# One masked step for the sign and low bits of the MLP's weights, and the low halves' subtraction shared out anew

## The chip, the cores and the metric

The kernel runs on one core of a Trainium2 chip. The metric is the device time of one execution in microseconds, as the median of several runs. The engines are TensorE (PE, its weight loads PEld), VectorE (DVE), ScalarE (ACT), GpSimd (POOL) and SyncE (SP), which issues most transfers. Each works through its own queue in order.

## What is computed

The reference chains three stages. Attention: 4 batches, 8 heads, 576 positions, 64 columns a head; half of the heads see the last 32 positions, the others every 32nd. Then an MLP over the 2304 tokens with 512 columns and 2048 hidden units, and then 8 experts of 1024 hidden units, of which each token takes one:

```python
def _moe_ref(x, w_in, w_out, alpha):
    h = x @ w_in
    g = np.maximum(h, 0.0) + alpha * np.minimum(h, 0.0)
    return g @ w_out
...
    e_idx = np.argmax(x @ w_gate, axis=1)
    ...
    h = np.maximum(x[mask] @ w1[e], 0.0)
    out[mask] = gate_w[mask, None] * eom[mask, e, None] * (h @ w2[e])
```

`w_in` and `w_out` are given as float64. The kernel reads the eight bytes of each number as they are and makes float32 numbers of them on the chip; this is the decoding that the change touches.

## The kernel before

**The MLP.** The hidden units are cut into 16 chunks of 128 (`NC1`), the tokens into 6 blocks of 384 (`NBLK`). For block `blk` and chunk `c` the step n = 16 blk + c makes `h` from the tokens (`mlp_in`, L439 to L441, on two PSUM banks `h`), applies the activation (`mlp_act`: L448 and L449 on ScalarE, L450 on VectorE), splits the result into a high and a low part (`mlp_split`: `gh` on ScalarE, L459, `gl` on VectorE, L460) and multiplies it with the second matrix (`mlp_out`, L473 to L475, on three accumulators). Every product is made of three: high by high, high by low, low by high. `mlp_in` and the activation run two steps ahead of `mlp_out`.

**The weights.** Chunk c of both matrices comes as one tile `raw` of 128 x 1024 float64 (1 MB, `load_w`, L391): columns 0 to 511 belong to `w_in`, 512 to 1023 to `w_out`. Each number is two 32-bit words, the low one (`words(c)[0]`) and the high one (`words(c)[1]`). Decoding takes four steps. `decode_a` (L402, ScalarE) copies the high word into a tile `stage`, scaled as a float32 by a power of two, which keeps its mantissa bits as they are. `decode_b` (VectorE) shifts the result left by 3 (L406) and brings in the top 3 bits of the low word, shifted right by 29 (L407). `decode_s` (L413, VectorE) brings in the sign from the high word. `decode_c` copies the result, rounded to the matrix format, into the high half of the tile `w` (L421, ScalarE), and GpSimd subtracts it for the low half (L422). `stage` has three buffers. The same kind of subtraction serves the experts' weights later (L886 to L888).

**The order** is written out by hand (`manual_schedule`): each engine's queue is the order of the calls. In 13 passes ahead of the loop (`NPRO`), attention's groups 0 to 9 are worked off, and chunk k's decoding starts in pass 2 + 2k and goes on by one step a pass (`T0`, chunks 0 to 4; `DEC` is 4). Then come the first two activations, and then the loop over n. In its first 12 passes, pass n ends the decoding of chunk n + 4, does `decode_b` and `decode_s` of chunk n + 5 and `decode_a` of chunk n + 6. In the same block attention's groups 10 to 22 go on, one in most passes. For a group, `att_scores` writes two banks (L228, L234), `att_max` takes maxima on VectorE (L252), `att_exp` makes exponentials on ScalarE (L278, L281), `att_norm` makes reciprocals on VectorE (L295, L296) and products on GpSimd (L297; one group on VectorE), `att_transpose` turns them on TensorE (L313, in the loop into bank `T`; read by L315), `att_values` multiplies with `v` (L328, in the loop into bank `T` as well) and `att_store` and `att_rest` split the result (`xh` on ScalarE, L367, `xl` on VectorE, L372). After the first block the weights stay in place.

Routing and the experts follow in the last block and behind it.

Of the kernel before, what the change touches and what calls it, by code (L numbers as in the profile page):

```python
# [7 lines left out]
F32 = mybir.dt.float32  # L8
F32R = mybir.dt.float32r
BF16 = mybir.dt.bfloat16  # L10
I32 = mybir.dt.int32
AF = mybir.ActivationFunctionType
ALU = mybir.AluOpType
X = mybir.AxisListType.X
# [9 lines left out]
NC1 = FF // P  # L24
# [18 lines left out]
DEC = 4  # L43
# [19 lines left out]
RS = 7  # L63
NEG = -1.0e9
BIG = 12582912.0
SIGN = -(2**31)

C_ID = 0
C_I8 = C_ID + P
# [14 lines left out]
def attention_prelu_mlp_routed_experts_kernel(  # L84
# [11 lines left out]
    nc = tc.nc  # L96
# [28 lines left out]
    with tc.manual_schedule():  # L125
# [144 lines left out]
        def att_exp(gi):  # L270
# [6 lines left out]
            if b < PE_MASK:  # L277
                nc.scalar.activation(out=nm[:r, : 2 * nj], in_=nm[:r, : 2 * nj], func=AF.Copy, scale=SCALE)  # L278
            for u in range(2 * nj):
# [3 lines left out]
                    in_=src,  # L283
                    func=AF.Exp,
                    bias=nm[:r, u : u + 1],
# [18 lines left out]
        def att_transpose(gi, tag):  # L304
# [9 lines left out]
            ptt = apool.tile([P, 4, P], F32, tag="pt", name="ptt", bufs=NPT_BUFS)  # L314
            nc.scalar.activation(out=ptt[:kk, :nu, :r], in_=tr[:kk, :nu, :r], func=AF.Copy)  # L315
            pt_t[gi] = ptt
# [20 lines left out]
        def att_store(gi):  # L337
# [28 lines left out]
            for src, dh, dl in moves:  # L366
                nc.scalar.activation(out=dh, in_=src, func=AF.Copy)  # L367
            px_t[gi] = moves
# [8 lines left out]
        raw_t, w_t = {}, {}  # L377

        def stage():
            return xpool.tile([P, 2 * (DM + 1)], F32, tag="stage", name="stage", bufs=3)  # L380
# [3 lines left out]
        def w_tile(c, dt, name):  # L384
            return wpool.tile(
                [P, 2048], dt, tag="wa" if c < NA else "wb", name=name, bufs=NA if c < NA else NC1 - NA
            )

        def load_w(c):
            raw_t[c] = w_tile(c, I32, "raw64")  # L390
            nc.sync.dma_start(raw_t[c], wp[c].bitcast(I32))  # L391


        dec_t = {}

        def words(c):
            two = raw_t[c].rearrange("p (n two) -> p n two", two=2)
            return two[:, :, 0], two[:, :, 1]

        def decode_a(c):  # L400
            t = dec_t[c] = stage()[:, :1024]
            nc.scalar.activation(out=t, in_=words(c)[1].bitcast(F32), func=AF.Copy, scale=2.0**-112)  # L402

        def decode_b(c):
            t = dec_t[c].bitcast(I32)
            nc.vector.tensor_scalar(out=t, in0=t, scalar1=3, scalar2=None, op0=ALU.logical_shift_left)  # L406
            nc.vector.scalar_tensor_tensor(  # L407
                out=t, in0=words(c)[0], scalar=29, in1=t, op0=ALU.logical_shift_right, op1=ALU.bitwise_or
            )

        def decode_s(c):
            t = dec_t[c].bitcast(I32)
            nc.vector.scalar_tensor_tensor(  # L413
                out=t, in0=words(c)[1], scalar=SIGN, in1=t, op0=ALU.bitwise_and, op1=ALU.bitwise_or
            )
            raw_t.pop(c)

        def decode_c(c):
            t = dec_t.pop(c)
            w = w_t[c] = w_tile(c, F32R, "w")  # L420
            nc.scalar.activation(out=w[:, :1024], in_=t, func=AF.Copy)  # L421
            nc.gpsimd.tensor_tensor(out=w[:, 1024:], in0=t, in1=w[:, :1024].bitcast(F32), op=ALU.subtract)  # L422

        def w_in(c, part, k):
            return w_t[c][:, part * 1024 + k * P : part * 1024 + (k + 1) * P]
# [29 lines left out]
        def mlp_split(n):  # L455
            v = h_t.pop(n)
            gh = xpool.tile([P, BLK], F32R, tag="gh", name="gh", bufs=3)
            gl = xpool.tile([P, BLK], F32R, tag="gl", name="gl", bufs=2)
            nc.scalar.activation(out=gh, in_=v, func=AF.Copy)  # L459
            nc.vector.tensor_tensor(out=gl, in0=v, in1=gh.bitcast(F32), op=ALU.subtract)  # L460
            g_t[n] = (gh, gl)
# [606 lines left out]
        def load_ws(k):  # L1068
            for _, c in zip(range(k), loads):
                load_w(c)  # L1070
# [49 lines left out]
        steps_done = {}  # L1120

        def decode(k, n):

            steps = [decode_a, decode_b, decode_s, decode_c]
            for f in steps[steps_done.get(k, 0) : n]:
                f(k)
            steps_done[k] = max(steps_done.get(k, 0), min(n, 4))

        for s in range(NPRO):
            att_step(s, ("h", "h") if s % 2 else ("S", "X"), "acc0" if s % 2 else "T", "acc1" if s % 2 else "acc2")  # L1130
# [4 lines left out]
            if s == 4:  # L1135
# [3 lines left out]
                    out=wg_hl[:, :, 2 * E :], in0=wg_sb, in1=wg_hl[:, :, : 2 * E].bitcast(F32), op=ALU.subtract  # L1139
                )  # L1140
                nc.vector.memset(acc_oh[:, 0, :], 0.0)
            for k in range(NC1):
                n = s - (T0[k] if k < len(T0) else 99)
                if n >= 0:
                    decode(k, n + 1)

        span[:] = [FIRST + EXTRA if EXTRA < LV else 0, NG]
        decode(DEC, 3)
        decode(DEC + 1, 1)
        for n in range(2):  # L1150
            mlp_in(n, range(KD - 1, KD))
            mlp_act(n)
            mlp_split(n)
        last = NBLK * NC1
        turn_at, logits_at = {}, {}
        for blk in range(NBLK - 1):
            for j in range(TPB):
                c = 2 * j + 1 if blk < NBLK - 2 else j
# [11 lines left out]
        for n in range(last):  # L1170
            blk, c = divmod(n, NC1)
            todo = []
            if blk + 1 < len(steps_of) and c < NC1 - 2:
                s0, s1 = steps_of[blk + 1]
                k = s1 - s0
                todo = list(range(s0 + k * c // (NC1 - 2), s0 + k * (c + 1) // (NC1 - 2)))
            for s in todo[:-1]:
                att_step(s, ("S", "X"), "T", "T")
            s = todo[-1] if todo else -9
            if on(s - 1):  # L1180
                att_exp(s - 1)
                att_norm(s - 1)
            if n + 2 < last:
                mlp_in(n + 2)
            if on(s - LV):
                att_values(s - LV, "T")
                att_store(s - LV)
            att_back(s)
            if n + 2 < last:
                mlp_act(n + 2)  # L1190
            if n + DEC < NC1:
                decode(n + DEC, 4)
            att_front(s)
            if on(s):
                att_scores(s, ("S", "X"))
                att_max(s)
            if n + DEC + 1 < NC1:
                decode(n + DEC + 1, 3)
            mlp_out(n, range(1))
            if on(s - LT):  # L1200
                att_transpose(s - LT, "T")
            mlp_out(n, range(1, 2))
            if (blk - 1, c) in logits_at:
                logits(blk - 1, logits_at[blk - 1, c])
            if (blk - 1, c) in turn_at:
                turn(blk - 1, turn_at[blk - 1, c])
            if blk > 0 and c == (7 if blk < NBLK - 1 else 4):
                gather_logits(blk - 1)
                rest = route_parts(blk - 1)
                next(rest)  # L1210
            if blk > 0 and c == (8 if blk < NBLK - 1 else 5):
                next(rest, None)
            if blk > 0 and c == (9 if blk < NBLK - 1 else 6):
                rank(blk - 1)
            mlp_out(n, range(2, TPB))
            load_ws(1)
            if n + DEC + 2 < NC1:
                decode(n + DEC + 2, 1)
            if n + 2 < last:
                mlp_split(n + 2)  # L1220
            if c == NC1 - 1 and blk == 3:
                s_a.close()
                epool = s_x.enter_context(tc.tile_pool(name="epool", bufs=1))
                idx_in = epool.tile([P, NSLOT], I32, name="idx_in")
                idx_out = epool.tile([P, NSLOT], I32, name="idx_out")
                idx_any = epool.tile([1, 1], I32, name="idx_any")
                e_i32 = epool.tile([1, NSLOT], I32, name="e_i32")
                taken = epool.tile([P, NTT], F32, name="taken")
                used = epool.tile([P, E], F32, name="used")
                nc.vector.memset(taken, 0.0)  # L1230
            if blk == NBLK - 1:
                if c == 6:
                    for _ in plan_parts(True):
                        pass
                    load_expert(0, 0)
                    load_expert(0, 1)
                if c == EL:
                    lists(True)
                    indices(True)
                if c in (9, 10, 11):  # L1240
                    gathers(0)
                if c == 11:
                    split_expert(0, 0)
                    load_expert(1, 0)
                if c == 13:
                    turn_x(0, 0)
                if c == 14:
                    turn_x(0, 1, bank("X"))
                    gathers(2)
                    split_expert(1, 0)  # L1250
                    load_expert(2, 0)
                if c == 15:
                    turn_x(1, 0)
            if c == NC1 - 1:
                evacuate(blk)
# [236 lines left out]
```

## Time and profile before

| | |
|---|---|
| median of 3 runs | 828.43 us (828.38 to 828.44) |
| profiled execution | 827.54 us, its span 825.8 us |
| granted TensorE clock, mean | 0.978 |
| TensorE busy | 783.3 us, 95% |
| VectorE busy | 465.1 us, 56% |
| ScalarE busy | 427.6 us, 52% |
| GpSimd busy | 223.9 us, 27% |

The profile shows one execution. A row of a timeline has the start and the duration in us, the engine, the line of the kernel (L406), the operation, its output and inputs by the program's names, their shapes, and in brackets the idle time of the engine just before it with what ended it. A busy time counts from an instruction's start to its end, with any time in which it stands still in between. Instructions of one engine can overlap by about 0.1 us at their ends. The granted clock is given as a share of TensorE's full 2.4 GHz. Rows with "..." between them leave lines out.

### The profile page before, as it was taken

The numbers are of one execution on the slowest core, as the hardware profiler recorded it, in microseconds if no ns is written. First come the engines' busy times: TensorE is split into PE (matmuls) and PEld (weight loads), VectorE is DVE, ScalarE is ACT, GpSimd is POOL, SyncE is SP. The second block draws the span as 40 slices with busy tenths as digits, with TensorE's granted clock in tenths as the row PEclk, the third lists the DMA queues.
The fourth block names the chain that finished last, engine by engine and source line by source line (L and its number), as shares of the span: only waits on it lengthen the run. The fifth ranks groups of instructions, "written<-read, shape, count | busy, mean of one in ns | idle before, by whom it ended". The sixth has DMA issues, their size and how long they took to land. (4 is left out here: it accounts for less than half of the span.)

```text
span 825.8 us, 13693 instructions
## 1 busy us (share of the span) xinstructions
PE 783.3 (95%) x5035; PEld 659.0 (80%) x5035; DVE 465.1 (56%) x980; ACT 427.6 (52%) x1057; POOL 223.9 (27%) x152
## 2 busy tenths in 40 slices
PE   7778889999999999999999999999989998999996
PEld 4566767888888888888898898889879876878884
DVE  4979997345544454556333434657695447854422
ACT  6847676445544454555333333265534656655542
POOL 2734444011100011111000000113474465546422
PEclk9789899999999999999999999999999999999998
DMA  9707411111200121101000100553224577787421
GB/s 342 303 1 298 167 56 49 33 33 46 84 18 1 47 87 64 36 11 39 2 1 1 39 1 1 204 191 125 56 90 159 176 268 250 281 290 270 161 88 41
DMA packets 22621, 91.04 MB, mean 110 GB/s; under 512 B 3082, under 2 KB 7312, under 8 KB 15376
## 3 DMA queue, kind: packets, MB, share of 16 engines
q1 hardware_dynamic: 18816, 78.52, 26.8%
q0 software_dynamic: 3728, 11.55, 4.0%
q8 instruction: 41, 0.67, 0.3%
q14 instruction: 36, 0.29, 0.1%
HBM read 105.78 MB, written 9.97 MB: 140 GB/s over the span
## 5 line engine op out<-in xcount | busy, mean ns | idle before, releaser
L439 PE MATMUL h<-xh,w 128*128 128x384 f32 x384 | 131.2, 342 | 4.1 <-DVE gl L460 3.8
L440 PE MATMUL h<-xl,w 128*128 128x384 f32 x384 | 130.5, 340 | 0.7 <-DVE xl L372 0.7
L441 PE MATMUL h<-xh,w 128*128 128x384 f32 x384 | 130.4, 340 | 0.0
L450 DVE SCALAR_TENSOR_TENSOR h<-h,nalpha,a 128x384 f32<-128x384 f32 x96 | 59.9, 624 | 116.1 <-ACT h L449 116.0
L473 PE MATMUL acc<-w,gh 128*128 128x512 f32 x288 | 125.3, 435 | 0.0
L297 POOL TENSOR_TENSOR p<-p,sm 96x512 f32<-96x512 f32 (+2 forms) x47 | 48.2, 1026 | 283.6 <-DVE sm L296 260.5
L888 DVE TENSOR_TENSOR wx<-raw,wx 128x1024 fp32r<-128x1024 f32 x72 | 97.1, 1392 | 46.9 <-ACT wx L886 46.6
L475 PE MATMUL acc<-w,gl 128*128 128x512 f32 x288 | 114.3, 397 | 0.0
L474 PE MATMUL acc<-w,gh 128*128 128x512 f32 x288 | 114.1, 396 | 0.0
L448 ACT ACTIVATE a<-h 128x384 f32<-128x384 f32 x96 | 47.2, 491 | 105.9 <-PE h L441 105.9
L886 ACT ACTIVATE wx<-raw 128x1024 fp32r<-128x1024 f32 x96 | 94.6, 1056 | 7.6 <-DMA raw<-in_wexp_dram 7.6
L1042 PE MATMUL acc<-wx,hh 128*128 128x512 f32 x304 | 97.0, 401 | 0.0
L888 POOL TENSOR_TENSOR wx<-raw,wx 128x1024 fp32r<-128x1024 f32 x24 | 63.1, 2629 | 90.7 <-ACT wx L886 90.6
L439 PEld LDWEIGHTS h<-xh,w 128*128 128x128 f32 x384 | 73.4, 191 | 9.6 <-DVE gl L460 5.5
L440 PEld LDWEIGHTS h<-xl,w 128*128 128x128 f32 x384 | 73.2, 191 | 4.8 <-DVE xl L372 1.0
L441 PEld LDWEIGHTS h<-xh,w 128*128 128x128 f32 x384 | 73.2, 191 | 0.0
L460 DVE TENSOR_TENSOR gl<-h,gh 128x384 fp32r<-128x384 f32 x96 | 53.3, 555 | 33.0 <-PE acc L475 18.2
L895 POOL DMA_INDIRECT xg<-rows,idx_in x23 | 29.3, 1274 | 145.4 <-ACT h L449 139.0
L1042 PEld LDWEIGHTS acc<-wx,hh 128*128 128x128 f32 x304 | 56.6, 191 | 11.2
L475 PEld LDWEIGHTS acc<-w,gl 128*128 128x128 f32 x288 | 54.6, 190 | 13.2
L459 ACT ACTIVATE gh<-h 128x384 fp32r<-128x384 f32 x96 | 46.7, 486 | 34.8 <-DVE h L450 34.7
L473 PEld LDWEIGHTS acc<-w,gh 128*128 128x128 f32 x288 | 54.5, 189 | 10.6 <-issue 0.3
(259 smaller groups left out, 1548.3 us busy)
## 6 DMA issues: line engine op xcount, KB each, us to landing
raw<-in_wexp_dram SPq DMA_DIRECT2D x64, 1024.0 KB
raw<-in_wp_dram SPq DMA_DIRECT2D x16, 1024.0 KB
qk<-in_qkv_dram SPq DMA_DIRECT2D x10, 576.0 KB
rows<-stage SPq DMA_DIRECT2D x15, 256.5 KB
v<-in_qkv_dram SPq DMA_DIRECT2D x8, 320.0 KB
qk<-in_qkv_dram SPq DMA_DIRECT2D x4, 384.0 KB
v<-in_qkv_dram SPq DMA_DIRECT2D x6, 256.0 KB
qk<-in_qkv_dram SPq DMA_DIRECT2D x4, 224.0 KB
```

The lines of the kernel that those rows point to most:

```text
L297: (nc.vector if gi in NRV else nc.gpsimd).tensor_tensor(out=pt[:r, :nu, :kk], in0=pt[:r, :nu, :kk], in1=sm[:r, :nu].unsqueeze(2).to_broadc ...
L439: mm(ph[:, :BLK], w_in(c, 0, k), xh[:, k, :], start=(k == 0), stop=False)
L440: mm(ph[:, :BLK], w_in(c, 0, k), xl[:, k, :], start=False, stop=False)
L441: mm(ph[:, :BLK], w_in(c, 1, k), xh[:, k, :], start=False, stop=(k == KD - 1))
L450: nc.vector.scalar_tensor_tensor(out=v, in0=v, scalar=nalpha[:, c : c + 1], in1=a, op0=ALU.mult, op1=ALU.add)
L460: nc.vector.tensor_tensor(out=gl, in0=v, in1=gh.bitcast(F32), op=ALU.subtract)
L473: mm(o, gh[:, t], w_out(c, 0), start=(c == 0), stop=False)
L474: mm(o, gh[:, t], w_out(c, 1), start=False, stop=False)
L475: mm(o, gl[:, t], w_out(c, 0), start=False, stop=(c == NC1 - 1))
L886: nc.scalar.activation(out=w[:, :1024], in_=raw, func=AF.Copy)
L888: eng.tensor_tensor(out=w[:, 1024:], in0=raw, in1=w[:, :1024].bitcast(F32), op=ALU.subtract)
L1042: mm(po[i], h[:, h0 : h0 + P], wk[:, w0 : w0 + 512], start=st, stop=sp)
```

## The change

`decode_b` no longer reads the low word as 32 bits. A shift on 16-bit parts takes the second 16 bits of each number, shifts them right by 13 and writes the 3 bits over the low 16 bits of the high word in `raw` itself (`decode_a` has read that word before). The shift left by 3 stays. `decode_s` then takes the sign and the 3 bits from the high word with one mask, in one instruction as before. So VectorE's L407, on 1024 words, gives way to a 16-bit instruction on 1024 elements, and L413 keeps its form with another constant.

The low half is made in two parts by a new function `low`. For chunks 0 to 3, VectorE subtracts all 1024 columns, in a fifth step `decode_d`, one pass after `decode_c`. For chunks 4 to 15, GpSimd subtracts the columns of `w_out` in `decode_c`, and VectorE those of `w_in` in `decode_d`, which stands in pass n behind `mlp_out` and `load_ws`, ahead of `decode_a` of chunk n + 6 and of `mlp_split`. The calls `decode(DEC, 3)` and `decode(DEC + 1, 1)` move from ahead of the first two activations to behind them.

```diff
--- before.py
+++ after.py
@@ -9,6 +9,7 @@
 F32R = mybir.dt.float32r
 BF16 = mybir.dt.bfloat16
 I32 = mybir.dt.int32
+U16 = mybir.dt.uint16
 AF = mybir.ActivationFunctionType
 ALU = mybir.AluOpType
 X = mybir.AxisListType.X
@@ -63,7 +64,7 @@
 RS = 7
 NEG = -1.0e9
 BIG = 12582912.0
-SIGN = -(2**31)
+SIGN_AND_TAIL = -(2**31) + 7
 
 C_ID = 0
 C_I8 = C_ID + P
...
@@ -403,23 +406,34 @@
 
         def decode_b(c):
             t = dec_t[c].bitcast(I32)
+            q = raw_t[c].bitcast(U16).rearrange("p (n four) -> p n four", four=4)
+            nc.vector.tensor_scalar(
+                out=q[:, :, 2], in0=q[:, :, 1], scalar1=13, scalar2=None, op0=ALU.logical_shift_right
+            )
             nc.vector.tensor_scalar(out=t, in0=t, scalar1=3, scalar2=None, op0=ALU.logical_shift_left)
-            nc.vector.scalar_tensor_tensor(
-                out=t, in0=words(c)[0], scalar=29, in1=t, op0=ALU.logical_shift_right, op1=ALU.bitwise_or
-            )
 
         def decode_s(c):
             t = dec_t[c].bitcast(I32)
             nc.vector.scalar_tensor_tensor(
-                out=t, in0=words(c)[1], scalar=SIGN, in1=t, op0=ALU.bitwise_and, op1=ALU.bitwise_or
+                out=t, in0=words(c)[1], scalar=SIGN_AND_TAIL, in1=t, op0=ALU.bitwise_and, op1=ALU.bitwise_or
             )
             raw_t.pop(c)
 
+        def low(eng, c, a, b):
+            w = w_t[c]
+            eng.tensor_tensor(
+                out=w[:, 1024 + a : 1024 + b], in0=dec_t[c][:, a:b], in1=w[:, a:b].bitcast(F32), op=ALU.subtract
+            )
+
         def decode_c(c):
-            t = dec_t.pop(c)
             w = w_t[c] = w_tile(c, F32R, "w")
-            nc.scalar.activation(out=w[:, :1024], in_=t, func=AF.Copy)
-            nc.gpsimd.tensor_tensor(out=w[:, 1024:], in0=t, in1=w[:, :1024].bitcast(F32), op=ALU.subtract)
+            nc.scalar.activation(out=w[:, :1024], in_=dec_t[c], func=AF.Copy)
+            if c >= DEC:
+                low(nc.gpsimd, c, 512, 1024)
+
+        def decode_d(c):
+            low(nc.vector, c, 0, 512 if c >= DEC else 1024)
+            dec_t.pop(c)
 
         def w_in(c, part, k):
             return w_t[c][:, part * 1024 + k * P : part * 1024 + (k + 1) * P]
@@ -1121,10 +1135,10 @@
 
         def decode(k, n):
 
-            steps = [decode_a, decode_b, decode_s, decode_c]
+            steps = [decode_a, decode_b, decode_s, decode_c, decode_d]
             for f in steps[steps_done.get(k, 0) : n]:
                 f(k)
-            steps_done[k] = max(steps_done.get(k, 0), min(n, 4))
+            steps_done[k] = max(steps_done.get(k, 0), min(n, 5))
 
         for s in range(NPRO):
             att_step(s, ("h", "h") if s % 2 else ("S", "X"), "acc0" if s % 2 else "T", "acc1" if s % 2 else "acc2")
@@ -1145,12 +1159,12 @@
                     decode(k, n + 1)
 
         span[:] = [FIRST + EXTRA if EXTRA < LV else 0, NG]
-        decode(DEC, 3)
-        decode(DEC + 1, 1)
         for n in range(2):
             mlp_in(n, range(KD - 1, KD))
             mlp_act(n)
             mlp_split(n)
+        decode(DEC, 3)
+        decode(DEC + 1, 1)
         last = NBLK * NC1
         turn_at, logits_at = {}, {}
         for blk in range(NBLK - 1):
@@ -1214,6 +1228,8 @@
                 rank(blk - 1)
             mlp_out(n, range(2, TPB))
             load_ws(1)
+            if n + DEC < NC1:
+                decode(n + DEC, 5)
             if n + DEC + 2 < NC1:
                 decode(n + DEC + 2, 1)
             if n + 2 < last:
```

## Rows read from the trace of the kernel before

**Rows 1.** the page's busy us, share of the span and count, by engine:

```profile
PE 783.3 (95%) x5035; PEld 659.0 (80%) x5035; DVE 465.1 (56%) x980; ACT 427.6 (52%) x1057; POOL 223.9 (27%) x152
```

**Rows 2.** busy us by stretch, granted clock, DMA share, GB/s:

```profile
51.00:55.00 4.00, 3.92 (x12) 3.92 (x13) 1.21 (x3) 0.69 (x2) 0.00 (x0) 0.50 0.00 0
...
85.00:90.00 5.00, 5.00 (x17) 4.42 (x16) 4.93 (x6) 2.82 (x8) 3.23 (x2) 0.50 0.76 310
...
113.00:121.00 8.00, 6.45 (x47) 5.07 (x43) 7.86 (x12) 5.34 (x15) 3.85 (x2) 1.00 0.15 43
...
141.00:147.00 6.00, 6.00 (x45) 4.86 (x41) 2.53 (x7) 3.55 (x14) 0.85 (x2) 1.00 0.15 44
```

**Rows 3.** TensorE's waits: us in total, times, longest; the last from 8 to 140 us:

```profile
PE T L313 <- DVE xl L372: 8.2, 7, 2.3
...
PE sl_bank L228 <- ACT p L281: 1.7, 3, 0.6
...
PE X L228 <- ACT p L281: 1.3, 3, 0.5
...
PE h L439 <- DVE gl L460: 3.7, 1, 3.7
```

**Rows 4.** timeline of VectorE, one step: start, duration, line, operands:

```profile
101.56 0.41 DVE L252 TENSOR_REDUCE nm<-X 126x2 f32<-126x252 f32 x1
...
101.88 2.65 DVE L406 TENSOR_SCALAR stage<-stage 128x1024 int32<-128x1024 int32 x1
...
104.57 1.22 DVE L407 SCALAR_TENSOR_TENSOR stage<-raw,stage 128x1024 int32<-128x1024 int32 x1
...
105.83 1.22 DVE L413 SCALAR_TENSOR_TENSOR stage<-raw,stage 128x1024 int32<-128x1024 int32 x1
...
107.44 0.16 DVE L295 TENSOR_SCALAR sm<-sm 126x4 f32<-126x4 f32 x1
...
108.78 0.41 DVE L252 TENSOR_REDUCE nm<-X 126x2 f32<-126x252 f32 x1
```

**Rows 5.** timeline of GpSimd, the same step:

```profile
101.57 2.42 POOL L422 TENSOR_TENSOR w<-stage,w 128x1024 fp32r<-128x1024 f32 x1
```

**Rows 6.** timeline of VectorE, stalls ahead of the loop and in its first pass:

```profile
24.28 2.05 DVE L295 TENSOR_SCALAR sm<-sm 126x4 f32<-126x4 f32 x1
...
32.87 0.81 DVE L295 TENSOR_SCALAR sm<-sm 126x4 f32<-126x4 f32 x1 [0.78 <-ACT p L281]
...
39.43 2.33 DVE L295 TENSOR_SCALAR sm<-sm 72x2 f32<-72x2 f32 x1
...
46.20 3.18 DVE L413 SCALAR_TENSOR_TENSOR stage<-raw,stage 128x1024 int32<-128x1024 int32 x1
...
57.55 3.34 DVE L407 SCALAR_TENSOR_TENSOR stage<-raw,stage 128x1024 int32<-128x1024 int32 x1
```

**Rows 7.** one line's instructions: shortest, median, longest in ns:

```profile
L406 DVE TENSOR_SCALAR stage<-stage x16: 675/804/2997, 14.3 to 130.6; 128x1024 int32<-128x1024 int32 x16
...
L422 POOL TENSOR_TENSOR w<-stage,w x16: 2355/2498/3350, 23.0 to 137.6; 128x1024 fp32r<-128x1024 f32 x16
...
L888 DVE TENSOR_TENSOR wx<-raw,wx x72: 1210/1220/3426, 543.8 to 807.6; 128x1024 fp32r<-128x1024 f32 x72
```

**Rows 8.** timeline of VectorE, where steps of the loop begin:

```profile
63.05 0.40 DVE L252 TENSOR_REDUCE nm<-sl_bank 96x2 f32<-96x256 f32 x1
...
137.12 0.41 DVE L252 TENSOR_REDUCE nm<-sl_bank 96x2 f32<-96x256 f32 x1
...
143.05 0.41 DVE L252 TENSOR_REDUCE nm<-sl_bank 96x2 f32<-96x256 f32 x1
...
149.23 0.41 DVE L252 TENSOR_REDUCE nm<-sl_bank 96x2 f32<-96x256 f32 x1
```

**Rows 9.** timeline of ScalarE at the moved call:

```profile
44.98 1.20 ACT L402 ACTIVATE stage<-raw 128x1024 f32<-128x1024 f32 x1
...
46.91 0.49 ACT L448 ACTIVATE a<-h 128x384 f32<-128x384 f32 x1 [0.73 <-PE h L441]
```


## The prediction

> **What bounds the kernel now.** I began with the page's busy shares: TensorE 95%, VectorE 56%, ScalarE 52%, GpSimd 27% [rows 1]. They suggest that a change on VectorE and GpSimd is worth nothing. The shares by stretch say otherwise, and this is the first thing to see: from 113 to 121 us VectorE is busy for 7.86 of 8 us and TensorE for 6.45, while from 141 to 147 us, with the weights decoded, VectorE has 2.53 of 6 and TensorE is full [rows 2]. So the change can act only in about the first 140 us; behind them TensorE is the bound and an earlier start is kept to the end.
>
> The second view is TensorE's waits between 62 and 140 us: 8.2 us for VectorE's `xl` (L372) and 1.7 and 1.3 us for ScalarE's exponentials [rows 3]. All three stand behind VectorE: the transpose needs the bank that L372 empties, and the exponentials need the maxima (L252), which VectorE does late. That is 11.2 us. Before them lies one wait of 3.7 us for `gl` (L460) [rows 3], right ahead of the stretch from 51 us. After that gap, and after the longest wait for `xl`, 2.3 us, the granted clock is 0.50, the 1.2 GHz level, for some 4 to 5 us (51 to 55, 85 to 90) [rows 2].
>
> The third view is VectorE's timeline over one step. One step of the loop runs from the maxima at 101.56 to those at 108.78: 7.22 us, with no gap [rows 4]. In it L406, the shift by 3, takes 2.65 us; its shortest is 0.675 [rows 4, 7]. It stands from just after GpSimd's L422 began (101.57, for 2.42 us) [rows 5] until 0.55 us behind its end. So 1.97 us of the 7.22 are not work: VectorE stands still while GpSimd subtracts. The same is seen on L295, L413 and L407 elsewhere, each far above its unhindered time [rows 6].
>
> The Trainium skill gives a name to that (SBUF, section Who interferes with whom): VectorE and GpSimd share one pair of ports, held for a whole instruction by whoever comes first; the trace agrees by 2.65 us against 0.675.
>
> **The change, part by part: one step of the loop.** Per chunk, GpSimd's subtraction shrinks from 1024 columns to 512; its price lies between 1.18 us (half of the shortest, 2.355) and 2.36 (nothing gained) [rows 7]. The work is plain streaming, so I take 1.25.
>
> VectorE loses L407, 1.26 us from start to next start [rows 4], and the stall, 1.97. What is left of its step is 7.22 - 1.97 - 1.26 = 3.99 us. It gains half of the subtraction: 1.21 for 1024 columns in the expert stage [rows 7], so between 0.61 and, with a fixed part, 0.68; I take 0.65. That makes 4.64. The new half stands behind L413 and ahead of `gl` (L460); its input from ScalarE is ready long before, since GpSimd starts from the same copy some 5 us earlier [rows 4, 5].
>
> The unknown is the 16-bit shift, x. No row shows a 2-byte operand at an 8-byte step. Below, the dense shift L406: 0.72 from start to start without its stall. Nearest is L407 itself: it reads words of the same tile at the same 8-byte step, 1.22 us [rows 4]. An upper end I take from that row doubled, 2.46, should two-byte writes cost twice. Which port it takes matters too. At 1.23 without the shared ports it fills the time in which GpSimd holds them: GpSimd starts 0.31 us ahead of VectorE's decoding [rows 4, 5] and has 0.94 left, so L406 behind it waits for nothing and the step is 4.64 + 1.23 = 5.87 us. At 0.72 with the ports it waits those 0.94: 4.64 + 0.72 + 0.94 = 6.30 us. The ends nearly cancel, which is why I trust the sum more than either price.
>
> By the Trainium skill (VectorE: DVE Perf Modes, section What auto-detection actually checks) one source and a destination in SBUF with an even count suffice for the two-port mode, whatever the step; that would be the case of 6.30, and no run here shows it yet.
>
> **TensorE's floor.** Ten steps run from 63.05 to 137.12 us, 7.41 each [rows 8]. Less the 11.2 us of waits [rows 3] and half of the 5 us at 0.50 [rows 2], they hold 60.4 us of TensorE's own, 6.04 each; the step without decoding, 143.05 to 149.23, takes 6.18 [rows 8]. So TensorE's floor is about 6.1, VectorE's 5.87 to 6.30. With two engines that close I take the larger, 6.3. The loop gives 10 x (7.41 - 6.3) = 11.1 us; between 13 at TensorE's floor and, with x at 2.46 (a step of 7.1), 3.
>
> **The part ahead of the loop.** Here chunks 0 to 3 are subtracted on VectorE wholly, 4 x 1.21 = 4.8 us more on its queue, ahead of the next chunk's L413 and, in the last pass, of the first activation (L450). What goes are four stalls behind L422: L295 2.05, 0.81 and 2.33 us for 0.16, and L413 3.18 for 1.22 [rows 4], together 1.89 + 0.65 + 2.17 + 1.96 = 6.7 [rows 6]. GpSimd's softmax products (L297) no longer queue behind L422, which helps TensorE, but I price that at nothing since VectorE is the fuller queue there. At x = 1.23 the shift costs what L407 did. So 6.7 - 4.8 = 1.9 us gained before the loop; from 0 (VectorE stalls behind L297 instead) to 4 (x = 0.72 on five chunks as well). In the loop's first pass L407 stands 3.34 us for 1.23 [rows 6]: 2.1 of stall become some 0.6, and 0.65 of subtraction comes in: 0.9 gained. Together 2.8.
>
> The moved calls: `decode(DEC, 3)` does nothing at either place, since the passes before have done those steps; `decode(DEC + 1, 1)` is one ScalarE copy, at 44.98, that ends before the activation at 46.91 starts, which waits for TensorE [rows 9]. Behind both activations it meets a ScalarE that waits for TensorE's next product. Without that cover it would cost its 1.2 us once. Nothing else in the queues moves; SP's loads keep their order, and follow TensorE's earlier release of the buffers.
>
> **Sum.** 11.1 + 2.8 = 13.9 us. The profiled execution took 827.54 us, 0.9 under the median 828.43; 827.54 - 13.9 = 813.6, so 814.5 as a median.
>
> **The rivals.** (a) VectorE stays the bound: GpSimd's half hardly shrinks, or begins later and meets L406 or L413 with its full length, a stall of about 1 us a step. For it: L407 and L413 are hit as well as L406 [rows 6]. Against: the shift ahead of them lengthens the head start. A step of 6.9, 5.1 from the loop, 1.9 before: 821.5. (b) More than the sum: TensorE at its floor, 10 x 1.3 = 13, and the gap before 51 us closes enough that its stretch at 0.50 goes, 2 us: with 2.8, 17.8, 810.6. Against: about 2 us of that gap remain, and a wait on `xl` of little over 2 us was enough for the drop at 85 us. (c) The other side: two-byte writes into four-byte words are slow. The loop gives 10 x (7.41 - 4.64 - x) and the part before it 2.8 - 5 x (x - 1.23), which is nothing together at x = 2.4 us; beyond, the kernel is slower. At 3.7, three times the nearest row, it loses 9.3 + 9.6 = 19: 847. For it: no row shows such a write. Against: at that step L407 and L413 read in 1.22 us [rows 4] what the dense L888 reads in 1.21 at best [rows 7]. (d) Nothing changes: x about 2.4, gains and costs cancelling, 828.
>
> **How the numbers follow.** The forecast (812 to 818) 0.62; (a) 0.16; (b) 0.13; (c) 0.06; (d) 0.03. The range 810 to 821 takes in (b), the forecast and most of (a). Over 0.2%, 1.7 us, is what a measurement of this kernel can tell: faster 0.91, within it 0.03, slower 0.06.
>
> **What would show it.** Right: the new shift lasts 0.7 (with a stall) or about 1.2 us; GpSimd's subtraction about 1.25, twelve of them; maxima 6.1 to 6.4 us apart in the loop; TensorE's wait for `xl` under 3 us; no 0.50 at the place of 85 us; the first L450 about 2 us earlier. Wrong: the shift above 2 us; L406 or L413 still near 2 to 3 us; VectorE still full with steps above 6.7; or steps bounded by a ScalarE wait that the queue of before hid.

## The result and the profile after

The changed kernel takes 819.62 us as the median of four runs (819.08 to 820.06) against 828.43. That is 8.8 us less, where 13.9 were forecast; 819.62 lies inside the stated range. The ratio, of the means of the runs, is 0.9885 (95% interval 0.9862 to 0.9907); that of the medians is 0.9894, since a fourth run of the kernel before took 831.42. The profiled execution took 819.41 us with a span of 817.6. Lines are numbered anew: the shift left is L413 now (was L406), the masked step L417 (L413), the subtraction L424 on either engine (L422), the activation L464 (L450), `xl` L373 (L372), the maxima L253 (L252), the transpose L314 (L313). The new 16-bit shift is L410.

Busy time by stretch of the kernel after (stretch, its length, busy us of PE, PEld, DVE, ACT and POOL, granted clock, DMA share, GB/s):

```profile
51.00:55.00 4.00, 4.00 (x18) 3.64 (x16) 1.10 (x3) 2.45 (x4) 0.00 (x0) 0.79 0.00 0
80.00:84.00 4.00, 4.00 (x15) 3.42 (x14) 3.97 (x5) 2.82 (x8) 2.51 (x2) 0.58 1.02 424
...
113.00:121.00 8.00, 7.82 (x56) 5.86 (x53) 7.90 (x19) 7.05 (x20) 2.18 (x3) 1.00 0.20 53
130.00:136.00 6.00, 6.00 (x44) 4.86 (x43) 2.89 (x9) 3.37 (x14) 1.04 (x1) 1.00 0.16 48
```

VectorE is still full while weights are decoded, 7.90 of 8 us from 113 to 121, but TensorE now has 7.82 there against 6.45 in [rows 2]. From 130 us on VectorE is free and TensorE full. A stretch mostly at the 1.2 GHz level remains: the granted clock is 0.58 from 80 to 84 us.

TensorE's waits in the loop, 58 to 140 us (total, times, longest):

```profile
PE T L314 <- DVE xl L373: 5.2, 6, 2.4
PE X L229 <- ACT p L282: 0.7, 2, 0.4
PE sl_bank L229 <- ACT p L282: 0.5, 1, 0.5
```

The wait for `xl` is 5.2 us against 8.2 [rows 3]; its longest, 2.4 us, stands right ahead of the stretch at 0.58.

VectorE's timeline, one row of an earlier step and parts of two steps of the loop:

```profile
66.88 2.54 DVE L410 TENSOR_SCALAR raw<-raw 128x1024 uint16<-128x1024 uint16 x1
...
73.31 0.41 DVE L253 TENSOR_REDUCE nm<-X 126x2 f32<-126x252 f32 x1
73.64 1.34 DVE L410 TENSOR_SCALAR raw<-raw 128x1024 uint16<-128x1024 uint16 x1
74.77 1.76 DVE L413 TENSOR_SCALAR stage<-stage 128x1024 int32<-128x1024 int32 x1
...
79.97 0.22 DVE L253 TENSOR_REDUCE nm<-X 72x1 f32<-72x72 f32 x1
...
94.94 0.41 DVE L253 TENSOR_REDUCE nm<-X 126x2 f32<-126x252 f32 x1
95.27 2.18 DVE L410 TENSOR_SCALAR raw<-raw 128x1024 uint16<-128x1024 uint16 x1
97.25 0.71 DVE L413 TENSOR_SCALAR stage<-stage 128x1024 int32<-128x1024 int32 x1
98.00 1.23 DVE L417 SCALAR_TENSOR_TENSOR stage<-raw,stage 128x1024 int32<-128x1024 int32 x1
99.14 0.68 DVE L424 TENSOR_TENSOR w<-stage,w 128x512 fp32r<-128x512 f32 x1
...
101.55 0.41 DVE L253 TENSOR_REDUCE nm<-X 126x2 f32<-126x252 f32 x1
```

and GpSimd's, the same three steps and one product ahead of the loop:

```profile
14.41 2.13 POOL L298 TENSOR_TENSOR p<-p,sm 96x512 f32<-96x512 f32 x1 [2.72 <-DVE sm L297]
...
66.97 1.29 POOL L424 TENSOR_TENSOR w<-stage,w 128x512 fp32r<-128x512 f32 x1
...
73.72 2.25 POOL L424 TENSOR_TENSOR w<-stage,w 128x512 fp32r<-128x512 f32 x1
...
94.95 1.30 POOL L424 TENSOR_TENSOR w<-stage,w 128x512 fp32r<-128x512 f32 x1
```

These are the rows to look at. In the step at 73 us the shift L410 runs first and GpSimd waits for it (2.25 us for 1.29), then L413 waits for GpSimd: 1.76 us for 0.72. In the step at 95 us GpSimd comes first and L410 itself waits, 2.18 us, with 1.98 to the next start against 1.13 at 73 us. So a step still holds about 1 us in which VectorE stands still: 0.85 to 1.22 us in eight of the ten steps, 0.17 and 0.48 in the other two. The starts alone do not tell which engine will wait: at 66.97 GpSimd begins 0.09 us behind the shift and runs its 1.29 us while the shift takes 2.54; at 73.72 it begins 0.08 us behind and waits. What decides it was not sought. Ahead of the loop the same holding up shows from the other side: at 14.41 GpSimd's product takes 2.13 us, as long as the shift beside it (1.09 from its start to the next, at 15.53) plus its own 1.03:

```profile
14.44 1.30 DVE L410 TENSOR_SCALAR raw<-raw 128x1024 uint16<-128x1024 uint16 x1
```

Shortest, median and longest of the three new or halved kinds, in ns:

```profile
L410 DVE TENSOR_SCALAR raw<-raw x16: 1295/1392/2544, 14.4 to 121.9; 128x1024 uint16<-128x1024 uint16 x16
...
L413 DVE TENSOR_SCALAR stage<-stage x16: 712/1140/1776, 15.5 to 123.0; 128x1024 int32<-128x1024 int32 x16
...
L424 POOL TENSOR_TENSOR w<-stage,w x12: 1289/1589/3312, 55.3 to 128.5; 128x512 fp32r<-128x512 f32 x12
```

The starts that mark the parts (the first activation, and the maxima of the first and the eleventh step, beside [rows 6, 8]):

```profile
47.71 0.62 DVE L464 SCALAR_TENSOR_TENSOR h<-h,nalpha,a 128x384 f32<-128x384 f32 x1
...
60.51 0.41 DVE L253 TENSOR_REDUCE nm<-sl_bank 96x2 f32<-96x256 f32 x1
...
127.94 0.41 DVE L253 TENSOR_REDUCE nm<-sl_bank 96x2 f32<-96x256 f32 x1
```

The first activation starts at 47.71 us, where in [rows 6] the stall ahead of it ends at 49.38; the loop's first maxima 2.54 earlier (63.05 to 60.51), and ten steps take 67.43 us, 6.74 each, against 7.41.

### The profile page after: what moved, and what is told of

Read it like the earlier page. It is cut to its first block, busy times and chain, and to the rows that moved or that the text cites. A ratio compares the mean times of both kernels' runs of the same rounds, so it can differ in the third digit from the quotient of the medians.

```text
span 817.6 us, 13679 instructions
## 1 busy us (share of the span) xinstructions
PE 779.1 (95%) x5032; PEld 656.3 (80%) x5035; DVE 458.4 (56%) x996; ACT 427.2 (52%) x1057; POOL 204.8 (25%) x148
## 4 chain that ended last, share of the span: by engine, by line
PE 77%; DVE 12%; issue 4%; ACT 4%; POOL 1%; DMA 0%; SPq 0%; POOLq 0%; ACTq 0%; DVEq 0%
PE acc L1056 10%; PE acc L487 8%; PE h L453 7%; PE h L455 7%; PE h L454 7%; PE acc L489 7%; PE acc L488 7%; PE T L329 2%; PE sl_bank L235 2%; DVE wx L902 2%; PE T L314 2%; DVE raw L410 2%; PE h L979 1%; PE h L981 1%; PE h L980 1%
## 5 line engine op out<-in xcount | busy, mean ns | idle before, releaser
L464 DVE SCALAR_TENSOR_TENSOR h<-h,nalpha,a 128x384 f32<-128x384 f32 x96 | 59.9, 624 | 115.8 <-ACT h L463 115.7
```

Of the source, the lines that this page charges most:

```text
L464: nc.vector.scalar_tensor_tensor(out=v, in0=v, scalar=nalpha[:, c : c + 1], in1=a, op0=ALU.mult, op1=ALU.add)
```

## The experiments

Two theories stood against each other. Theory 1: VectorE's queue sets the step, and the shift is both dear (1.12 us from start to start; 1.29 of duration, of which the next instruction overlaps the end) and in the way of GpSimd, so the stall that the forecast let vanish beside a dear shift stays. Theory 2: a chain over ScalarE and TensorE's bank `T` sets the step, and VectorE's stall is cover. In the table, "first" is the start of the first activation on VectorE, "step" the mean over the ten steps of [rows 8], both from the profiled run; the ratio is to the kernel before, with its interval. Below the first row, where no ratio stands, there was one run.

| run | first | step | us | ratio |
|---|---|---|---|---|
| before | 49.30 | 7.41 | 828.43 | |
| the change | 47.71 | 6.74 | 819.62 | 0.9885 (0.9862 to 0.9907) |
| the change once more | 48.73 | 6.75 | 820.00 | 0.9903 (0.9887 to 0.9918) |
| all subtraction on VectorE | 48.49 | 6.50 | 816.95 | 0.9853 (0.9833 to 0.9872) |
| the same once more | 47.11 | 6.29 | 814.83 | 0.9842 (0.9825 to 0.9858) |
| masked step alone | 49.65 | 7.20 | 827.73 | 0.9986 (0.9970 to 1.0002) |
| shares alone | 48.72 | 6.64 | 820.60 | 0.9899 (0.9879 to 0.9919) |
| 32-bit shift | 46.53 | 6.16 | 813.65 | |
| 16-bit shift, neighbouring elements | 45.48 | 6.04 | 810.13 | |
| no 16-bit shift | 46.37 | 6.03 | 811.17 | |
| multiplication for the shift | 47.82 | 6.74 | 820.66 | 0.9912 (0.9890 to 0.9935) |
| multiplication, all on VectorE | 47.89 | 6.29 | 816.94 | 0.9875 (0.9856 to 0.9894) |
| old call order | 47.12 | 6.61 | 819.30 | 0.9908 (0.9884 to 0.9932) |
| first chunks on GpSimd, others VectorE | 49.98 | 6.30 | 817.57 | 0.9872 (0.9853 to 0.9891) |

**All subtraction on VectorE.**

```diff
-            if c >= DEC:
-                low(nc.gpsimd, c, 512, 1024)
...
-            low(nc.vector, c, 0, 512 if c >= DEC else 1024)
+            low(nc.vector, c, 0, 1024)
```

> GpSimd subtracts nothing in the decoding; VectorE takes all 1024 columns for chunks 4 to 15 too. Theory 1 (VectorE's queue sets the step, and each step holds about 1.0 us in which it stands behind GpSimd's subtraction): the step is 3.99 + 1.12 for the 16-bit shift + 1.15 for the subtraction = 6.26 us against 6.74 in the changed kernel; ten steps give 4.8 us, so about 814.8 us, and the pair of shifts takes 1.9 us from the first's start to L417's, in every step. Theory 2 (the step is set by a chain over ScalarE and TensorE's bank T, VectorE's stall is cover): no stall to win back, 0.5 us more work on VectorE a step, 6.8 to 7.2 us, 820 to 824.

Measured 816.95 us and steps of 6.50. More work on VectorE, and yet a shorter step: theory 2's 820 to 824 is out. The step was 0.24 above theory 1's 6.26; this profile has a stretch at a granted clock of 0.76, from 73 to 80 us, which its repetition below does not have. The two shifts take 1.9 us together, as expected (67.94 to 69.83).

**The masked step alone.** The subtraction stays on GpSimd for every chunk.

```diff
-            if c >= DEC:
-                low(nc.gpsimd, c, 512, 1024)
+            low(nc.gpsimd, c, 0, 1024)
...
-            low(nc.vector, c, 0, 512 if c >= DEC else 1024)
...
+            pass
```

> The masked step alone; the whole subtraction stays on GpSimd for all 16 chunks, as before. Theory 1: the step is 3.99 + 1.12 + a stall of about 2.0 = 7.1 us against 7.41 before the change, 3 us from the loop; ahead of the loop 5 x 0.1 and the old stalls stay, so 824 to 826 us. Theory 2: the step stays near 6.74, since the subtraction on GpSimd is cover, about 820.

Measured 827.73 us, an interval that includes no change, and steps of 7.20. Theory 1's step (7.1) is near; its time, 824 to 826, was some 2 us too low. A stall of about 2 us is still there, on L413 in the loop's first pass and on L417 in the second:

```profile
58.31 2.89 DVE L413 TENSOR_SCALAR stage<-stage 128x1024 int32<-128x1024 int32 x1
...
65.92 3.26 DVE L417 SCALAR_TENSOR_TENSOR stage<-raw,stage 128x1024 int32<-128x1024 int32 x1
```

**The shares alone.** The old shift and or (L407 of before) with the new shares of the subtraction.

```diff
-SIGN_AND_TAIL = -(2**31) + 7
+SIGN_AND_TAIL = -(2**31)
...
-            nc.vector.tensor_scalar(
-                out=q[:, :, 2], in0=q[:, :, 1], scalar1=13, scalar2=None, op0=ALU.logical_shift_right
...
+            nc.vector.scalar_tensor_tensor(
+                out=t, in0=words(c)[0], scalar=29, in1=t, op0=ALU.logical_shift_right, op1=ALU.bitwise_or
+            )
```

> The old decoding (32-bit shift and or, no 16-bit shift) with the new shares of the subtraction. Theory 1: the step is 3.99 + 1.26 + 0.65 + a stall of about 1.0 = 6.9 us, so 5 us from the loop and 2.5 ahead of it: about 821 us; the masked step is then worth 1 to 2 us of the 8.8, the shares the rest. A rival: the masked step is the greater part, and this run stays above 825.

Measured 820.60 us and steps of 6.64, within the intervals the same as the whole change. I had expected the masked step to be worth 1 to 2 us; none of it shows, though intervals this wide would hide as much.

**A 32-bit shift at the same step.**

```diff
-SIGN_AND_TAIL = -(2**31) + 7
+SIGN_AND_TAIL = -(2**31)
...
-                out=q[:, :, 2], in0=q[:, :, 1], scalar1=13, scalar2=None, op0=ALU.logical_shift_right
+                out=words(c)[0], in0=words(c)[0], scalar1=29, scalar2=None, op0=ALU.logical_shift_right
```

> The 16-bit shift is replaced by one on whole 32-bit words at the same 8-byte step, in place in the low word (the 3 lowest bits are then left out of the weights). If the 8-byte step makes the 16-bit shift cost 1.12 us instead of the dense 0.72: 1.1 to 1.3 us here as well, and the step stays at 6.7. If the 2-byte elements do: 0.68 us here, a step of 6.3, and a time some 4 us under the changed kernel. GpSimd held up beside it for as long as it runs would show that it holds the shared ports.

The shift on 4-byte words, at the same 8-byte step, takes 0.68 us at its shortest:

```profile
L409 DVE TENSOR_SCALAR raw<-raw x16: 680/786/1934, 15.2 to 114.8; 128x1024 int32<-128x1024 int32 x16
```

and it holds GpSimd up too. VectorE and GpSimd in one step of this run:

```profile
70.77 0.69 DVE L409 TENSOR_SCALAR raw<-raw 128x1024 int32<-128x1024 int32 x1
71.37 1.79 DVE L412 TENSOR_SCALAR stage<-stage 128x1024 int32<-128x1024 int32 x1
```

```profile
70.86 1.76 POOL L423 TENSOR_TENSOR w<-stage,w 128x512 fp32r<-128x512 f32 x1
```

The step is 6.16 and the time 813.65 us. So the 8-byte step alone is not what made the 16-bit shift dear, and with a shift of 0.7 us the step comes out close to the forecast's 6.3.

**A multiplication that reads 4 bytes and writes 2.**

```diff
-                out=q[:, :, 2], in0=q[:, :, 1], scalar1=13, scalar2=None, op0=ALU.logical_shift_right
+                out=q[:, :, 2],
+                in0=words(c)[0].bitcast(U32),
+                scalar1=2.0**-29,
+                scalar2=-0.5,
+                op0=ALU.mult,
+                op1=ALU.add,
```

> The 3 bits are made by an arithmetic instruction in place of the 16-bit shift: it reads the whole 32-bit low word, multiplies by 2 to the -29, takes off one half, and rounds into the same 16-bit place (now and then one unit of the last place off). Reads are 4 bytes, writes 2 bytes, the step stays 8 bytes. If writing 2-byte elements is what makes the 16-bit shift take 1.12 us: about 1.1 to 1.3 us again, a step of 6.7 us, 819 to 820 us. If reading them is: 0.7 us, a step of 6.2 as with the 32-bit shift, about 814 us.

```profile
L411 DVE TENSOR_SCALAR raw<-raw x16: 1293/1392/2542, 14.5 to 122.0; 128x1024 uint16<-128x1024 uint32 x16
```

1.29 us, as the 16-bit shift, and steps of 6.74. So reading whole words does not make the instruction cheap while it writes 2-byte elements at the 8-byte step. That the writes are the cause is likely and not fully shown: this run also changes the operation, and what such a multiplication costs when it writes 4-byte elements was not measured.

**The multiplication, with all subtraction on VectorE.** This is the edit above and that of the first experiment together.

> The same, and the whole subtraction on VectorE, so that GpSimd holds nothing up. If the instruction takes 0.7 us: VectorE's step is 3.99 + 0.72 + 1.15 = 5.9 us, under TensorE's floor of 6.1, so about 6.1 to 6.2 and 813 us. If it takes 1.1 us: the step of the run with all subtractions on VectorE, 6.5 us, 816 to 817 us.

Measured 816.94 us and 6.29. The time is that of the second case; the step lies between the cases, and the instruction again takes 1.29 us at its shortest, so it is dear.

**A 16-bit shift over neighbouring elements.**

```diff
-SIGN_AND_TAIL = -(2**31) + 7
+SIGN_AND_TAIL = -(2**31)
...
-                out=q[:, :, 2], in0=q[:, :, 1], scalar1=13, scalar2=None, op0=ALU.logical_shift_right
+                out=q[:, 0:1024], in0=q[:, 0:1024], scalar1=0, scalar2=None, op0=ALU.logical_shift_right
```

with `q` the tile as 16-bit elements, unsplit.

> In place of the 16-bit shift stands a 16-bit shift by 0 over 1024 neighbouring elements of the same tile, and the mask takes the sign alone (the 3 lowest bits are left out of the weights). If writing 2-byte elements is slow by itself: about 1.3 us again, steps of 6.7. If it is slow only at the 8-byte step: 0.3 to 0.7 us, steps of 6.1 to 6.2 and 811 to 814 us.

```profile
L410 DVE TENSOR_SCALAR raw<-raw x16: 412/418/1664, 14.9 to 112.5; 128x1024 uint16<-128x1024 uint16 x16
```

0.41 us: 2-byte elements are fast side by side. Among these runs 1.29 came only where 2-byte elements were written at the 8-byte step. Steps of 6.04 and 810.13 us agree with a cheap shift.

**No 16-bit shift.**

```diff
-SIGN_AND_TAIL = -(2**31) + 7
+SIGN_AND_TAIL = -(2**31)
...
-            nc.vector.tensor_scalar(
-                out=q[:, :, 2], in0=q[:, :, 1], scalar1=13, scalar2=None, op0=ALU.logical_shift_right
-            )
```

> The 16-bit shift is left out and the mask takes the sign alone (the 3 lowest bits are left out of the weights); the shares of the subtraction stay. Theory 1 (VectorE's queue sets the step): 4.64 us plus a stall of about 1.0 behind GpSimd = 5.6, under TensorE's floor, so steps of 6.1 to 6.2 and 812 to 814 us. Theory 2 (a chain over other engines sets the step at 6.7): steps stay above 6.5, 818 us or more.

Measured 811.17 us and steps of 6.03, in which TensorE is full from 106 to 118 us:

```profile
106.00:118.00 12.00, 12.00 (x81) 9.72 (x80) 11.56 (x23) 9.90 (x34) 3.97 (x4) 1.00 0.15 40
```

That is TensorE's floor; the forecast had worked it out as 6.04 to 6.18 from waits and the low clock.

**The call order of before.**

```diff
+        decode(DEC, 3)
+        decode(DEC + 1, 1)
         for n in range(2):
             mlp_in(n, range(KD - 1, KD))
             mlp_act(n)
             mlp_split(n)
-        decode(DEC, 3)
-        decode(DEC + 1, 1)
```

> The changed kernel with the two moved calls back ahead of the first two activations. Expected: no difference, 819 to 820.5 us, the first activation on VectorE within 0.3 us of the changed kernel's 47.71. A rival: ScalarE's copy of 1.2 us now delays the first activation by as much, 821 us.

Measured 819.30 us, as expected, and a first activation at 47.12, 0.6 us earlier and not within 0.3: still within what the same code shows from run to run. The move costs and brings nothing that these runs can tell.

**The first chunks on GpSimd, and the best version once more.**

```diff
-            if c >= DEC:
-                low(nc.gpsimd, c, 512, 1024)
+            if c < DEC:
+                low(nc.gpsimd, c, 0, 1024)
...
-            low(nc.vector, c, 0, 512 if c >= DEC else 1024)
+            if c >= DEC:
+                low(nc.vector, c, 0, 1024)
```

> Chunks 0 to 3 are subtracted by GpSimd as before the change, chunks 4 to 15 by VectorE wholly; this prices the part ahead of the loop by itself. By the prediction (four stalls of 6.7 us against 4.8 us of work on VectorE): the first activation about 1.9 us later than in the run with everything on VectorE (about 49.6 to 50), and the time 1 to 2 us above it, 818 to 819. A rival: the stalls there are cover for waits on other engines, the first activation comes within 0.5 us and the time does not move.

> The kernel with the whole subtraction on VectorE once more. If it is really ahead of the changed kernel: 816 to 817.5 us, ratio 0.985 to 0.987, steps of 6.3 to 6.5 us; if the first comparison was chance, within 1 us of the changed kernel.

> The changed kernel once more, beside the next one on the same chip: 819 to 820 us, ratio 0.988 to 0.990, steps of 6.7 us.

Measured beside each other: 817.57, 814.83 and 820.00 us; the first two are 0.4 and 1.2 us under what was expected. The kernel with all subtraction on VectorE is ahead of the change, their intervals apart here (0.9825 to 0.9858 against 0.9887 to 0.9918; in the first comparison they overlapped), and it is the fastest of those that make the full weights. In its steps nothing on VectorE stands still, the shift takes its 1.14, L413 0.76, L417 1.14 and the whole subtraction 1.14 from start to start, 6.17 from one maximum to the next at 97.72 and 103.89, where the mean is 6.29:

```profile
97.72 0.41 DVE L253 TENSOR_REDUCE nm<-X 126x2 f32<-126x252 f32 x1
98.05 1.35 DVE L410 TENSOR_SCALAR raw<-raw 128x1024 uint16<-128x1024 uint16 x1
99.19 0.72 DVE L413 TENSOR_SCALAR stage<-stage 128x1024 int32<-128x1024 int32 x1
99.95 1.23 DVE L417 SCALAR_TENSOR_TENSOR stage<-raw,stage 128x1024 int32<-128x1024 int32 x1
101.09 1.22 DVE L424 TENSOR_TENSOR w<-stage,w 128x1024 fp32r<-128x1024 f32 x1
102.23 0.55 DVE L472 TENSOR_TENSOR gl<-h,gh 128x384 fp32r<-128x384 f32 x1
...
103.89 0.22 DVE L253 TENSOR_REDUCE nm<-X 72x1 f32<-72x72 f32 x1
```

and GpSimd has the softmax products alone:

```profile
96.92 1.03 POOL L298 TENSOR_TENSOR p<-p,sm 126x504 f32<-126x504 f32 x1 [5.47 <-DVE sm L297]
103.24 1.03 POOL L298 TENSOR_TENSOR p<-p,sm 126x504 f32<-126x504 f32 x1 [5.29 <-DVE sm L297]
```

With GpSimd's subtraction ahead of the loop the first activation comes at 49.98 instead of 47.11 (48.49 in the earlier run): its stalls there were no cover. The time is 2.7 us above the run beside it but 0.6 above the earlier one, and the intervals overlap, so what the part ahead of the loop is worth in time is not pinned down better than that.

## Why the prediction was right, and what was mis-sized

**What bounds the kernel**: right. VectorE's queue set the step, with about 2 us a step in which it stood behind GpSimd. (One of the ten steps after the change, that from 79.83 us at the low clock, is an exception: 7.79 us, in which VectorE itself waited for 0.93.) Theory 2 fell with the run that leaves the 16-bit shift out and with that which gives VectorE more work: steps of 6.03 and of 6.29 to 6.50, both under 6.74. A gain made in the first 140 us is kept, too: 9.19 us at the end of the decoding (149.23 [rows 8] against 140.04) and 9.18 at the block's last activation near 540 us.

**GpSimd's half**: 1.29 us against 1.25 forecast. **VectorE's half**: 0.68 of duration, 0.60 from start to start, against 0.65. Both right.

**The 16-bit shift**: here the sum failed. It took two cases together, dear without the shared ports (5.87 us a step) or cheap with them (6.30), and found that the ends nearly cancel. The chip has the third: dear with them. In the forecast's own terms that is 4.64 + 1.12 + 0.94 = 6.70. 4.64 + 1.12 is 5.76, and the measured 6.74 leaves 0.98 for the stall; the two steps shown above have 1.04 (1.76 less 0.72) and 0.85 (1.98 less 1.13). Over ten steps, 10 x (6.74 - 6.30) = 4.4 us of the loop's 11.1 did not come; 6.64 came. Where the shift is cheap, in the single 32-bit run, the step is 6.16 and the time 813.65, beside the forecast's 6.3 and 814.5. So the mechanism was right and the term x with its port was mis-sized. The rule named from the Trainium skill (VectorE: DVE Perf Modes, section What auto-detection actually checks) was borne out as to the ports, since GpSimd's product took 2.13 us beside the shift; the rate of a two-port instruction did not come with it, 1.12 us against 0.72.

In effect the case is close to rival (a), VectorE stays the bound at a step of 6.9. Of its two causes the first did not come, since GpSimd's half did shrink; the second did in five of the ten steps: GpSimd's half comes behind the shift and meets L413, the L406 of before (once L417, the L413 of before), with its full length, a stall of about 1 us. In the other five it holds up the shift itself. The slow-write rival (c) probably had the cause of the shift's price, 2-byte writes into four-byte words, at a smaller price than it needed: x = 1.12, not above 2.4.

**The signs and the range**: as said came the price of GpSimd's twelve halves and the earlier first activation. Not so came the steps (6.74, not 6.1 to 6.4), the wait for `xl` (5.2 us, not under 3) and the clock (below). One sign of being wrong came true, VectorE full with steps above 6.7, if barely. And 819.62 lies outside the forecast's own 812 to 818, which had the chance 0.62; the range holds it because it also took in most of rival (a).

**The part ahead of the loop**: 1.9 and 0.9 us forecast, 1.59 and 0.95 measured. Among the runs with VectorE's subtraction there and the dear shift, the first activation lies from 47.11 to 48.73, the mean of seven 47.84; with GpSimd's, at 49.65 and 49.98. That is 2.0 us, the forecast's 1.9. The spread of 1.6 us within the same code has its cause open.

**The low clock**: I expected none at the place of 85 us. It stayed, 0.58 from 80 to 84, behind a wait of 2.4 us for `xl`. The stretch from 51 us, which rival (b) let go, had 0.79 against 0.50. In the second run of the kernel with all subtraction on VectorE the longest wait for `xl` is 0.7 us, and TensorE has its full clock from 60 to 128 us:

```profile
PE T L314 <- DVE xl L373: 1.8, 4, 0.7
...
60.00:128.00 68.00, 65.41 (x428) 52.60 (x427) 65.13 (x121) 55.37 (x168) 10.14 (x11) 1.00 0.46 170
```

The first run of the same kernel has a wait of 1.7 us for ScalarE's exponentials, up to 71.80 us, and behind it a granted clock of 0.57 from 73 to 77. So such a stretch can come without a long wait for `xl`.

**The masked step**: the forecast swapped 1.26 us for 1.23 and saw its worth in leaving the ports to GpSimd. It does not leave them, and alone it moves the time by nothing that can be told from none (0.9970 to 1.0002, so up to 2.5 us are not ruled out).

**Open**: the profiled pair loses 1.05 us of the 9.18 behind 540 us, among the experts. The stretch from the 13th step's maxima to the end of the span lasts from 676.6 to 680.5 us in profiles of kernels that are the same there, so this is within their spread, with the kernel before at its lower end; what makes the spread was not sought.

## What to carry to other kernels

Price an instruction by its operands' size and step together: neither a row at the same step with 4-byte elements nor a row of 2-byte elements side by side gave the price of 2-byte elements 8 bytes apart. When the bound engine stands still behind another, taking the other's work over whole can be cheaper than sharing it out: 1.14 us of work replaced 0.60 of work and about 1 of stall. And when a sum seems safe because two unknown ends cancel, price the corner in which both are bad.

## What the runs showed of the hardware

VectorE's one-input instruction on 1024 elements a partition, at its shortest: 0.68 us for a shift of 4-byte elements, side by side or 8 bytes apart; 0.41 for 2-byte elements side by side; 1.29 for 2-byte elements 8 bytes apart, and 1.29 as well for the multiplication that reads 4 bytes and writes 2. The last two still hold GpSimd up for their whole time: beside them its product takes 2.13 and 2.12 us where it takes 1.03 alone. Whether 2-byte reads alone would cost as much no run shows. GpSimd's subtraction grows nearly with its columns, 1.29 us for 512 and 2.36 for 1024.
